# The second set's rows, turns and pair products inside the first set's inversion

## The chip, the cores and the metric

One core of a Trainium2 chip runs the kernel. The metric is the device time of one execution in microseconds, the median of several; an engine is TensorE (PE, with its weight loads as PEld), VectorE (DVE), ScalarE (ACT), GpSimd (POOL) or SyncE (SP, which here only issues DMAs).

## The reference

A recurrence over 768 steps for 4 batches x 8 heads, a 40 x 40 state each, and behind it two dense layers over the 3072 tokens of width 320 (hidden width 2048):

```python
for t in range(S):
    y[:, :, t] = np.einsum('bhd,bhde->bhe', rt, state)
    Sa = np.einsum('bhde,bhe->bhd', state, at)
    state = state * wt[:, :, None, :] - np.einsum('bhd,bhe->bhde', Sa, bt) + np.einsum('bhd,bhe->bhde', vt, kt)
h = x @ w_in                      # x: y as (3072, 320)
g = np.where(h >= 1, h, np.where(h <= -1, 0, (h + 1) ** 2 / 4))
out = g @ w_out
```

All data are fp32.

## The kernel before

The recurrence is done in 24 chunks of 32 steps (`L`). In a chunk the products of w up to each step turn the recurrence into matrix products: k and b are multiplied by the reciprocal products, a by the products (the rows `kt, P, at, bt`), and the steps' dependence on one another is a unit triangular 32 x 32 matrix for each head, made of the pair products of a and b, whose inverse `tinv` is needed. Four chunks are a set; there are six sets. For each set the rows are made, written to DRAM (`scr`), the pairs multiplied, the 32 x 32 matrices inverted (`invert`, 31 steps of a product L362 and a subtraction L368) and adopted by a transpose (L376).

The rows of sets 0 and 1 are made in one piece ahead of the loops (`early_rows`, a generator that the schedule advances): products of w (L172 to L177), a (L179, L180), reciprocals (L182, L184), then b and k (L186, L188). Their `at` and `bt` are turned on TensorE against an identity (`early_turn`, L199, four parts for each of the two), evicted by ScalarE (`early_evict`, L212), multiplied into pairs (`early_ab`, L223, evicted by L227) and stored chunk by chunk (`early_store`, L231, on SP's queue). r and v are copied to the same rows in DRAM by `copy_rv` (L138). Set 0 comes first, with its inversion on VectorE; set 1's inversion and those of the later sets are on GpSimd, a step at a time within windows.

The buffers of the early rows are borrowed: set 1's inputs lie in Xraw[0], Xraw[1], tiab and Yraw, its rows in wides[0] and its turned rows in wides[1], where set 0's rows were. The places of w_out's weights are opened later over both wides.

Every engine runs its instructions in the order in which the program writes them, and the whole order is written out by hand. `step_back("inv", 0)` advances set 0's inversion by a step (of 1, one VectorE instruction); the table `todo` says after which step something else is put in: `at(n, f)`. Behind the inversion comes the loop over chunks. In each chunk there are two halves of 16 heads (`hb`), each a `chain` of five stages: L519 with the copy L523; L529 with L536 and L540; L545 with L550, L556 with L563 and L568; L585 with L587. `turn` makes transposes on VectorE (L464, L467, L469), `scores` the products L485 and masks L497, `load_ti` and `load_cg` load the rows from DRAM, `shift` copies within a tile (L311). A chunk has four `fill`s. A fill has six slots; in each, the dense layers advance by 1280 columns (`feed`, once a group of 64 steps of y is there), one entry of the list `first` is taken (before: set 1's remaining rows, turns, pairs and stores), the weights advance by `PACE` steps (0.7 in the first ten fills, then 0.9), and the inversions, rows and pairs of later sets advance by their windows.

The dense layers run in 96 units (12 groups of tokens, eight each): `first` (L631), the gate (L639, L640, L642), a split into a rounded value and a rest (L648 on ScalarE, L649 on GpSimd) and `second` (L661). The weights arrive as eight-byte words whose bits are put together: a job (12 of w_in, 16 of w_out) is loaded raw on GpSimd's queue five jobs ahead (`AHEAD`, L711), two activations put its parts in staging places in Xraw (L723, L727), VectorE joins them (L731), ScalarE rounds (L743), and the rest is the subtraction L744, on VectorE for w_in and on GpSimd for w_out. Three pulls of `weights` are a job. The first unit needs 14 jobs done. With every third job of w_in L749 copies two parts on GpSimd's queue.

PSUM has four buffers for the recurrence (`psum`), two for `first` and two for `second`.

Of the kernel before, what the change touches and what calls it, by code (L numbers as in the profile page):

```python
# [9 lines left out]
F32 = mybir.dt.float32  # L10
# [23 lines left out]
AHEAD = 5  # L34
PACE = (0.7, 0.9)
# [19 lines left out]
def rwkv_moe_kernel(ctx: ExitStack, tc: tile.TileContext, r, k, v, w, a, b, w_in, w_out, ident_d, mask_d, out):  # L55
# [107 lines left out]
    def early_rows(s):  # L163
# [18 lines left out]
        nc.vector.reciprocal(rs[:, :, 7], Ps[:, :, 7])  # L182
        for t in range(7, 0, -1):
            nc.vector.tensor_mul(rs[:, :, t - 1], rs[:, :, t], ws[:, :, t])  # L184
        yield
        nc.vector.tensor_mul(bt, bl, rec)  # L186
        yield
        nc.vector.tensor_mul(kt, kl, rec)  # L188
# [158 lines left out]
    def invert(s):  # L347
# [5 lines left out]
        nc.gpsimd.memset(W, 0.0)  # L353
        nc.gpsimd.memset(W[:, 0:1024:33], 1.0)
# [359 lines left out]
    def weights():  # L714

        def start(k):
            m, n = sizes[k]
            words = raws[k][0:m]
            if jobs[k][0]:
                x, low = Xraw[1][0:m, n * ((k + 2) % 3) :][:, 0:n], Xraw[1][0:m, 3 * n : 4 * n]  # L720
            else:
                x, low = (y[0:m, n * ((k + 1) % 3) :][:, 0:n] for y in (Xraw[1], Xraw[0]))
# [14 lines left out]
        def split(k, x):  # L737
# [6 lines left out]
            (nc.gpsimd if kind else nc.vector).tensor_sub(lo, x, hi.bitcast(F32))  # L744
# [63 lines left out]
    load_ti(0, 1)  # L808
    for part in range(2):
        init_cg(1, part)  # L810
    load_cg(0, 1)
    for _ in range(2):
        next(rows_of[1])
    step_back("inv", 0)
    todo = {}
    at = lambda n, f: todo.setdefault(n, []).append(f)
    for c in range(1, 4):
        at(1, lambda c=c: early_store(0, c))
    for i in range(2):
        at(1, lambda i=i: copy_rv(0, i, 1, 3))  # L820
    for k in range(AHEAD):
        at(2, lambda k=k: raw_load(k))
# [5 lines left out]
    at(17, lambda: shift(0, 1))  # L828
    at(19, lambda: turn(0, 1, 0))
# [10 lines left out]
    gens = {}  # L840
# [3 lines left out]
    def turn_1(j, part):  # L844
        early_evict(1, j, part, early_turn(1, j, part))

    row = lambda: next(rows_of[1])
    steps = [[row], [], [row], [], [row], []]
    for part in range(4):
        steps[part + 1].append(lambda part=part: turn_1(0, part))  # L850
    steps += [[lambda part=part: turn_1(1, part)] for part in range(4)]
    steps += [[lambda half=half: early_ab(1, half)] for half in range(2)] + [[lambda: init_cg(2, 2)]]
    steps += [[lambda c=c: early_store(1, c)] for c in range(4)]
    steps += [[lambda i=i: copy_rv(1, i, 0, 4)] for i in range(2)] + [[lambda: pad_scr(1)]]
# [11 lines left out]

    def stage(c, hb):

        if (c, hb) in gens:
            next(gens[c, hb], 0)  # L870
# [103 lines left out]
```

## Time and profile before

| | us |
|---|---|
| median of 3 runs | 847.39 (845.87 to 848.33) |
| profiled execution, its own time | 853.33 |
| its span, first to last instruction | 851.4 |
| TensorE busy in it | 694.7 (82%) |
| VectorE | 592.5 (70%) |
| ScalarE | 477.5 (56%) |
| GpSimd | 444.8 (52%) |

The span has a start (the early rows, set 0's inversion to 64 us, three chunks without dense layers to some 152 us), a middle in which recurrence and dense layers share TensorE, and from about 800 us an end with dense layers alone. The profile gives for each instruction its start and duration and what ended the idle time of its engine before it. A share of busy time is a mean over stretches with different limits, so it is read by stretch.

### The profile page before, as it was taken

Reading aid. Unit: us, or ns where it says so; the run is one execution under the profiler, and the core shown is the slowest. Engines: PE = TensorE matmul, PEld = TensorE weight load, DVE = VectorE, ACT = ScalarE, POOL = GpSimd, SP = SyncE. Lnnn points to the kernel's source line nnn. Section 1 sums busy time; section 2 is a strip of 40 time slices with the busy share of each in tenths; the row PEclk is TensorE's granted clock in tenths of the full one; section 3 lists DMA queues with packets and bytes.
Section 4 is the critical chain, followed back from the end, with each engine's and each line's share of the span. In section 5 each row is a group of like instructions: output and inputs, shape, how many; then the busy total and the mean of one; then the engine's idle time right before and its main releaser. Section 6 shows DMA issues by size and latency. Waiting matters only on the chain.

```text
span 851.4 us, 35341 instructions
## 1 busy us (share of the span) xinstructions
PE 694.7 (82%) x15360; PEld 639.7 (75%) x15360; DVE 592.5 (70%) x1338; ACT 477.5 (56%) x1010; POOL 444.8 (52%) x623
## 2 busy tenths in 40 slices
PE   4334656687588867888998899999999999999994
PEld 4234645676577766778987789998899899999994
DVE  6796689978577845667777797787877678676210
ACT  5406466567554634545656466666566566655552
POOL 1300269986434777833778648775357743222331
PEclk9555566688887987878999899999999999999998
DMA  8798586875567545953538845434233334330100
GB/s 284 160 204 200 85 171 169 202 181 150 150 135 164 132 115 104 177 130 96 126 92 157 187 131 122 93 88 93 70 79 65 83 66 100 78 80 20 36 16 16
DMA packets 178450, 102.33 MB, mean 120 GB/s; under 512 B 123712, under 2 KB 171008, under 8 KB 178296
## 3 DMA queue, kind: packets, MB, share of 16 engines
q1 hardware_dynamic: 172024, 78.45, 42.3%
q0 software_dynamic: 6272, 21.63, 9.0%
q8 instruction: 121, 1.98, 1.0%
q14 instruction: 33, 0.27, 0.1%
HBM read 70.88 MB, written 27.53 MB: 116 GB/s over the span
## 4 chain that ended last, share of the span: by engine, by line
PE 49%; POOL 7%; DVE 6%; DMA 3%; ACT 3%; issue 2%; SPq 1%; ACTq 0%; POOLq 0%; DVEq 0%
PE ph L631 16%; PE po L661 15%; PE p L556 4%; PE p L545 3%; PE p L585 3%; PE p L485 2%; PE p L529 2%; PE p L519 2%; POOL lw L368 2%; POOL lw L362 2%; POOL gl L649 2%; PE p L334 1%; DMA lw<-scr 1%; DMA ld_w<-in_w_dram 1%; DMA scr<-arena 1%
## 5 line engine op out<-in xcount | busy, mean ns | idle before, releaser
L649 POOL TENSOR_TENSOR gl<-gt,gh 128x512 fp32r<-128x512 f32 x96 | 123.8, 1290 | 195.4 <-ACT gh L648 195.2
L631 PE MATMUL ph<-X,w 120*128 120x256 f32 x1536 | 222.8, 300 | 1.3 <-issue 1.3
L631 PEld LDWEIGHTS ph<-X,w 120*128 120x128 f32 x1536 | 202.3, 202 | 8.1 <-issue 1.3
L661 PE MATMUL po<-w,gh 128*128 128x320 f32 x768 | 134.4, 317 | 12.8 <-ACT gh L648 12.8
L642 DVE SCALAR_TENSOR_TENSOR gt<-gt,ph 128x512 f32<-128x512 f32 x96 | 65.6, 684 | 98.5 <-ACT gt L640 94.2
L661 PEld LDWEIGHTS po<-w,gh 128*128 128x128 f32 x768 | 117.5, 194 | 15.2 <-ACT gh L648 14.5
L639 ACT ACTIVATE gt<-ph,half_c 128x512 f32<-128x512 f32 x96 | 66.0, 688 | 65.3 <-PE ph L631 64.9
L661 PE MATMUL po<-w,gl 128*128 128x320 f32 x384 | 79.2, 330 | 19.7 <-POOL gl L649 19.7
L563 DVE SCALAR_TENSOR_TENSOR cg<-p,pr 40x160 f32<-40x160 f32 x184 | 59.1, 321 | 50.3 <-PE p L556 48.1
L368 POOL TENSOR_TENSOR lw<-lw 128x31 f32<-128x31 f32 (+15 forms) x155 | 88.5, 571 | 9.4
L362 POOL TENSOR_TENSOR lw<-lw 128x31 f32<-128x31 f32 (+15 forms) x155 | 82.7, 533 | 8.9
L497 DVE TENSOR_TENSOR cg<-p,mask 32x256 f32<-32x256 f32 x192 | 80.6, 420 | 3.5
L661 PEld LDWEIGHTS po<-w,gl 128*128 128x128 f32 x384 | 63.1, 199 | 24.1 <-POOL gl L649 23.7
L540 ACT ACTIVATE cg<-p 32x160 f32<-32x160 f32 x192 | 56.6, 295 | 40.1 <-PE p L529 22.1
L556 PE MATMUL p<-cg 128*64 128x72 f32 (+1 forms) x1536 | 66.4, 245 | 0.4 <-issue 0.4
L648 ACT CAST gh<-gt 128x512 fp32r<-128x512 f32 x96 | 59.6, 621 | 10.5 <-DVE gt L642 9.5
L550 ACT COPY ss<-p 40x320 f32<-40x320 f32 x92 | 38.6, 419 | 45.1 <-PE p L545 43.5
L640 ACT ACTIVATE gt<-gt 128x512 f32<-128x512 f32 x96 | 60.7, 632 | 3.1
L536 DVE SCALAR_TENSOR_TENSOR cg<-p,mask 32x128 f32<-32x128 f32 x192 | 55.3, 288 | 10.2 <-PE p L529 2.6
L556 PEld LDWEIGHTS p<-cg 128*64 128x64 f32 x1536 | 60.6, 154 | 0.9 <-issue 0.9
L585 PEld LDWEIGHTS p<-pr,ss 40*40 40x40 f32 x1472 | 36.1, 130 | 29.6 <-issue 25.2
L585 PE MATMUL p<-pr,ss 40*40 40x32 f32 x1472 | 41.2, 210 | 20.8 <-DVE pr L469 17.8
(97 smaller groups left out, 1121.2 us busy)
## 6 DMA issues: line engine op xcount, KB each, us to landing
ti<-scr SPq DMA_DIRECT2D x96, 200.0 KB
scr<-arena POOLq DMA_DIRECT2D x16, 640.0 KB, 5.6
cg<-scr SPq DMA_DIRECT2D x96, 80.0 KB
X<-Y SPq DMA_DIRECT2D x36, 160.0 KB
scr<-wide SPq DMA_DIRECT2D x8, 640.0 KB
w<-in_moe_w_out_dram POOLq DMA_DIRECT2D x16, 320.0 KB, 4.0
tiab<-scr SPq DMA_DIRECT2D x28, 160.0 KB
cg<-scr SPq DMA_DIRECT2D x96, 40.0 KB
```

The lines of the kernel that those rows point to most:

```text
L362: eng.tensor_mul(t3, W3[:, 0:n, j : j + 1].broadcast_to([128, n, m]), L3[:, j + 1 :, j].unsqueeze(1).broadcast_to([128, n, m]),)
L368: eng.tensor_sub(W3[:, 0:n, j + 1 :], W3[:, 0:n, j + 1 :], t3)
L497: nc.vector.tensor_tensor(out=cg[q, f::2, C_X : C_X + 64][:, 4 * i : 4 * i + 4].rearrange("p h (j x) -> p h j x", x=32), in0=ps[quarter(f, ...
L556: nc.tensor.matmul(psv[h // 8][64 * f : 64 * f + 64, h // 2 % 4, 0:n3], lhsT=cgw[:, h * CW + C_G : h * CW + C_G + 64], rhs=cg[:, h, C_R : ...
L585: nc.tensor.matmul(psv[er[f], p, :], lhsT=ss[er[f], p, :], rhs=pn[er[f], p, 0, 8:40], start=True, stop=True)
L631: nc.tensor.matmul(phs[k % 2][:, n * j : n * j + n], lhsT=wt[0, f // 4, wi // 2][:, wi % 2, fs], rhs=Xs[g][:, xi, :], start=i == 0, stop=i ...
L639: nc.scalar.activation(gt, ph, AF.Relu, bias=half_c, scale=0.5)
L640: nc.scalar.activation(gt, gt, AF.Square)
L642: nc.vector.scalar_tensor_tensor(out=gt, in0=gt, scalar=1.0, in1=ph, op0=ALU.min, op1=ALU.max)
L648: nc.scalar.copy(gh, gt)
L649: nc.gpsimd.tensor_sub(gl, gt, gh.bitcast(F32))
L661: nc.tensor.matmul(pos[i], lhsT=x[:, ts_], rhs=w, start=q == 0 and k == 0, stop=end)
```

## The change

Set 1's reciprocal products (L184) and its products with b and k (L186, L188) go to GpSimd, in nine pieces that are put in at steps 1 to 9 of set 0's inversion; its reciprocal (L182) is written just behind that inversion's first transpose. Its turns with their evictions are put in at steps 22 to 29 and its pair products at 58 and 60. In the loop their place in `first` is empty. Set 0's stores, and then the copies of r and v, are issued ahead of the inversion's steps, before the loads of chunk 0's second half; that half's shift comes at step 54 and its turn 0 in the loop. The first stage of chunk 0's first half comes at step 20. Set 1's stores are entries 12 to 15 of `first` (before 13 to 16), its copies of r and v 24 and 25 (before 17 and 18), and its one-row copy `pad_scr` is gone. Set 0's inversion has its start matrix made on ScalarE. The weights take 1.2 steps a slot in the first four fills, then 0.9; the subtraction of jobs 0 to 6 goes to GpSimd, and the staging places of w_in's jobs alternate between the two Xraw, four for one part and two for the other.

```diff
-PACE = (0.7, 0.9)
+PACE = (1.2, 0.9)
...
         nc.vector.reciprocal(rs[:, :, 7], Ps[:, :, 7])
+        eng = nc.gpsimd if s else nc.vector
+        if s:
+            yield
         for t in range(7, 0, -1):
-            nc.vector.tensor_mul(rs[:, :, t - 1], rs[:, :, t], ws[:, :, t])
+            eng.tensor_mul(rs[:, :, t - 1], rs[:, :, t], ws[:, :, t])
+            if s:
+                yield
+        if not s:
+            yield
+        eng.tensor_mul(bt, bl, rec)
         yield
-        nc.vector.tensor_mul(bt, bl, rec)
-        yield
-        nc.vector.tensor_mul(kt, kl, rec)
+        eng.tensor_mul(kt, kl, rec)
         yield
...
-        nc.gpsimd.memset(W, 0.0)
-        nc.gpsimd.memset(W[:, 0:1024:33], 1.0)
+        if s:
+            nc.gpsimd.memset(W, 0.0)
+            nc.gpsimd.memset(W[:, 0:1024:33], 1.0)
+        else:
+            zero(W)
+            nc.scalar.activation(
+                W[:, 0:1024:33], half_c.broadcast_to([128, 32]), AF.Copy, scale=2.0
+            )
...
-                x, low = (y[0:m, n * ((k + 1) % 3) :][:, 0:n] for y in (Xraw[1], Xraw[0]))
+                x, low = (Xraw[y][0:m, n * i : n * i + n] for y, i in (((1, 1), (0, 0), (1, 0), (0, 1))[k % 4], (1 - k % 2, 2)))
...
-            (nc.gpsimd if kind else nc.vector).tensor_sub(lo, x, hi.bitcast(F32))
+            (nc.gpsimd if kind or k < 7 else nc.vector).tensor_sub(lo, x, hi.bitcast(F32))
...
-    load_ti(0, 1)
-    for part in range(2):
-        init_cg(1, part)
-    load_cg(0, 1)
+    for c in range(1, 4):
+        early_store(0, c)
     for _ in range(2):
         next(rows_of[1])
     step_back("inv", 0)
+    for part in range(2):
+        init_cg(1, part)
+    load_ti(0, 1)
+    load_cg(0, 1)
+    for i in range(2):
+        copy_rv(0, i, 1, 3)
+    next(rows_of[1])
...
-    for c in range(1, 4):
-        at(1, lambda c=c: early_store(0, c))
-    for i in range(2):
-        at(1, lambda i=i: copy_rv(0, i, 1, 3))
-    for k in range(AHEAD):
-        at(2, lambda k=k: raw_load(k))
+    for k in range(9):
+        at(1 + k, lambda: next(rows_of[1]))
+        if k % 2 and k // 2 < AHEAD:
+            at(1 + k, lambda k=k: raw_load(k // 2))
+    for k in range(4, AHEAD):
+        at(6 + k, lambda k=k: raw_load(k))
...
-    at(17, lambda: shift(0, 1))
-    at(19, lambda: turn(0, 1, 0))
+    gens[0, 0] = chain(0, 0)
+    at(20, lambda: stage(0, 0))
+    for j in range(2):
+        for part in range(4):
+            at(22 + 4 * j + part, lambda j=j, part=part: turn_1(j, part))
+    at(54, lambda: shift(0, 1))
+    for half in range(2):
+        at(58 + 2 * half, lambda half=half: early_ab(1, half))
...
-    steps = [[row], [], [row], [], [row], []]
-    for part in range(4):
-        steps[part + 1].append(lambda part=part: turn_1(0, part))
-    steps += [[lambda part=part: turn_1(1, part)] for part in range(4)]
-    steps += [[lambda half=half: early_ab(1, half)] for half in range(2)] + [[lambda: init_cg(2, 2)]]
-    steps += [[lambda c=c: early_store(1, c)] for c in range(4)]
-    steps += [[lambda i=i: copy_rv(1, i, 0, 4)] for i in range(2)] + [[lambda: pad_scr(1)]]
+    steps = [[] for _ in range(3)] + [[lambda: init_cg(2, 2)]]
+    steps += [[] for _ in range(8)] + [[lambda c=c: early_store(1, c)] for c in range(4)] + [[] for _ in range(8)]
+    steps += [[lambda i=i: copy_rv(1, i, 0, 4)] for i in range(2)]
...
-            due[0] += PACE[now[0] >= 25]
+            due[0] += PACE[now[0] >= 10]
...
-            gens[c, 0] = chain(c, 0)
+            if c:
+                gens[c, 0] = chain(c, 0)
             gens[c, 1] = chain(c, 1)
         stage(c - 1, 1)
-        stage(c, 0)
+        if c:
+            stage(c, 0)
...
-            for j in (1, 2):
+            for j in (1, 2) if c else (1, 2, 0):
                 turn(c, 1, j)
```

## Rows read from the trace of the kernel before

**Rows 1.** Busy time in three stretches: PE, PEld, DVE, ACT, POOL, clock, DMA share.

```profile
34.00:64.00 30.00, 9.24 (x224) 8.11 (x224) 27.61 (x73) 3.53 (x8) 5.50 (x11) 0.56 1.00 209
64.00:85.00 21.00, 9.87 (x226) 8.71 (x226) 12.70 (x25) 14.85 (x28) 1.25 (x3) 0.57 0.85 202
...
500.00:600.00 100.00, 99.64 (x2449) 92.11 (x2447) 78.09 (x191) 64.50 (x143) 63.35 (x93) 0.98 0.46 107
```

**Rows 2.** Groups of instructions by line, VectorE, 33.55 to 61.7 us: busy, mean ns.

```profile
L368 DVE TENSOR_TENSOR lw<-lw 128x31 f32<-128x31 f32 (+15 forms) x31 | 10.6, 343 | 1.2
L362 DVE TENSOR_TENSOR lw<-lw 128x31 f32<-128x31 f32 (+15 forms) x31 | 10.6, 342 | 1.1
```

**Rows 3.** Timeline, 43 to 71 us: start, time, engine, instruction, what ended the wait.

```profile
43.74 0.90 DVE L464 STREAM_TRANSPOSE cg<-ti 64x256 f32<-64x256 f32 x2
...
61.73 1.91 DVE L376 STREAM_TRANSPOSE tinv<-lw 128x1024 f32<-128x1024 f32 x1
...
64.73 1.11 DVE L182 RECIPROCAL arena<-wide 128x160 f32<-128x160 f32 x1
65.87 2.48 DVE L184 TENSOR_TENSOR arena<-arena,X 128x160 f32<-128x160 f32 x7
...
70.17 0.45 PE L529 MATMUL p<-x,tinv 32*32 32x72 f32 x4 [17.42 <-ACT wide L212]
70.40 1.49 DVE L188 TENSOR_TENSOR wide<-Y,arena 128x1280 f32<-128x1280 f32 x1
```

**Rows 4.** Timeline, 77 to 91 us.

```profile
77.08 0.59 DVE L536 SCALAR_TENSOR_TENSOR cg<-p,mask 32x128 f32<-32x128 f32 x2 [0.30 <-ACT cg L540]
...
77.72 4.99 PE L199 MATMUL p<-pr,wide 128*40 128x64 f32 x96 [2.03 <-DVE cg L536]
...
90.27 0.95 PE L545 MATMUL p<-cg 128*40 128x40 f32 x21
```

**Rows 5.** Groups of instructions, ScalarE, whole span, shapes apart: busy, mean ns, idle before.

```profile
L212 ACT COPY wide<-p 40x512 f32<-40x512 f32 x16 | 9.3, 578 | 1.6 <-PE p L199 1.4
...
L727 ACT ACTIVATE X<-w 120x512 uint32<-120x512 uint8 x8 | 5.3, 663 | 20.4 <-DVE arena L184 20.4
```

**Rows 6.** Groups of instructions, GpSimd, whole span, shapes apart.

```profile
L649 POOL TENSOR_TENSOR gl<-gt,gh 128x512 fp32r<-128x512 f32 x96 | 123.8, 1290 | 195.4 <-ACT gh L648 195.2
...
L292 POOL TENSOR_TENSOR arena<-ld_b,wz 128x320 f32<-128x320 f32 x16 | 16.7, 1046 | 0.0
...
L368 POOL TENSOR_TENSOR lw<-lw 128x156 f32<-128x156 f32 x10 | 5.2, 520 | 0.6
```

**Rows 7.** VectorE's weight steps by shape; two of them and GpSimd's L649 in the timeline.

```profile
L731 DVE SCALAR_TENSOR_TENSOR X<-X 128x320 uint32<-128x320 uint32 x16 | 14.5, 908 | 2.6 <-ACT X L727 2.5
...
L731 DVE SCALAR_TENSOR_TENSOR X<-X,X 120x512 uint32<-120x512 uint32 x8 | 6.2, 779 | 0.0
L744 DVE TENSOR_TENSOR w<-X,w 120x512 fp32r<-120x512 f32 x8 | 6.0, 745 | 12.0 <-ACT w L743 11.9
...
179.89 3.24 DVE L731 SCALAR_TENSOR_TENSOR X<-X 128x320 uint32<-128x320 uint32 x1
183.76 0.49 DVE L731 SCALAR_TENSOR_TENSOR X<-X 128x320 uint32<-128x320 uint32 x1 [0.63 <-ACT X L727]
...
180.52 1.26 POOL L649 TENSOR_TENSOR gl<-gt,gh 128x512 fp32r<-128x512 f32 x1
```

**Rows 8.** TensorE in the timeline from 157 us; waits from 64 to 106 us.

```profile
157.21 1.54 PE L545 MATMUL p<-cg 128*40 128x40 f32 x31 [0.79 <-ACT cg L540]
...
171.21 1.43 PE L661 MATMUL po<-w,gl 128*128 128x320 f32 x4 [6.42 <-POOL gl L649]
...
POOL w L749 <- ACT w L743: 14.4, 1, 14.4
```

**Rows 9.** SP in the timeline; DMA issues, median us to landing last.

```profile
35.55 13.19 SPq L231 DMA_DIRECT2D scr<-wide  x3
...
w<-in_moe_w_in_dram POOLq DMA_DIRECT2D x16, 160.0 KB, 7.2
```

More of the change, by code (lines that the diff above doesn't have):

```diff
@@ L814, in rwkv_moe_kernel, with stage, turn_1 @@
     step_back("inv", 0)
+    for part in range(2):
[5 more added lines that the diff above has]
+    next(rows_of[1])
+    gens = {}
+    def stage(c, hb):
+        if (c, hb) in gens:
+            next(gens[c, hb], 0)
+    def turn_1(j, part):
+        early_evict(1, j, part, early_turn(1, j, part))
     todo = {}
     at = lambda n, f: todo.setdefault(n, []).append(f)
-    for c in range(1, 4):
-        at(1, lambda c=c: early_store(0, c))
-    for i in range(2):
-        at(1, lambda i=i: copy_rv(0, i, 1, 3))
-    for k in range(AHEAD):
-        at(2, lambda k=k: raw_load(k))
+    for k in range(9):
[4 more added lines that the diff above has]
+        at(6 + k, lambda k=k: raw_load(k))
     at(9, lambda: shift(0, 0))
@@ L839, in rwkv_moe_kernel @@
     mgen = moe()
-    gens = {}
     owed, idle = [0], [True]
@@ L843, in rwkv_moe_kernel @@
     due = [0]
-    def turn_1(j, part):
-        early_evict(1, j, part, early_turn(1, j, part))
-    row = lambda: next(rows_of[1])
-    steps = [[row], [], [row], [], [row], []]
-    for part in range(4):
-        steps[part + 1].append(lambda part=part: turn_1(0, part))
-    steps += [[lambda part=part: turn_1(1, part)] for part in range(4)]
-    steps += [[lambda half=half: early_ab(1, half)] for half in range(2)] + [[lambda: init_cg(2, 2)]]
-    steps += [[lambda c=c: early_store(1, c)] for c in range(4)]
-    steps += [[lambda i=i: copy_rv(1, i, 0, 4)] for i in range(2)] + [[lambda: pad_scr(1)]]
+    steps = [[] for _ in range(3)] + [[lambda: init_cg(2, 2)]]
+    steps += [[] for _ in range(8)] + [[lambda c=c: early_store(1, c)] for c in range(4)] + [[] for _ in range(8)]
+    steps += [[lambda i=i: copy_rv(1, i, 0, 4)] for i in range(2)]
     first = [lambda x=x: [f() for f in x] for x in steps]
@@ L865, in feed @@
             idle[0] = d is None
-    def stage(c, hb):
-        if (c, hb) in gens:
-            next(gens[c, hb], 0)
     def catch_up():
```

## The prediction, made before the changed kernel was run

> **What bounds the kernel now.** I read the busy time by stretch first [rows 1]. From 500 us on TensorE is busy 99.6 us in 100: whatever is won ahead of that arrives at the end unchanged, and nothing in the change touches what is done there. The start is different. From 34 to 64 us VectorE is busy 27.6 of 30 us, while TensorE, ScalarE and GpSimd do 9.2, 3.5 and 5.5: this is the first set's inversion on VectorE, 31 steps of a product and a subtraction at 0.34 us [rows 2], with the three others nearly idle beside it. From 64 to 85 no engine is busy for more than 71% of the time, so there something waits in a chain. The timeline [rows 3, 4] says what. The inversion's last transpose ends at 61.73 + 1.91 = 63.64 us. The next step of the recurrence on TensorE (L529) needs only that, but starts at 70.17: it has waited 17.4 us for the eviction L212 of the second set's turns, which stand ahead of it and hold the PSUM buffers. L212 stands on ScalarE behind L727, which writes a part of a staged weight into Xraw[0] and waited 20.4 us for L184, the second set's reciprocal products on VectorE: those read the same buffer and stand behind the inversion [rows 5]. After L529 the pattern repeats on TensorE: the masked results L536 are ready at 77.08 + 0.59 = 77.7, but L545, which takes them up, starts at 90.27, since 96 of the second set's turns (L199) and all its pair products (L223) are ahead of it in the queue. So 90.27 - 63.64 = 26.6 us pass between the end of the inversion and L545, and that is what the change attacks. After that come half-chunks of (157.21 - 90.27) / 5 = 13.4 us each [rows 4, 8] until the dense layers begin.
>
> **The change part by part.** The stretch from the inversion to L545. The turns, their 16 evictions and the pair products go inside the inversion, where TensorE and ScalarE are idle; the block of ScalarE at L727 falls away, since Xraw[0] is free earlier and the first job no longer stages there. I cost them at nothing: their cover is the inversion, some 28 us, against 9.3 us of evictions [rows 5] and less of TensorE. What remains from the last transpose to L545 is what stood from L529 to the end of L536 before, 77.7 - 70.2 = 7.5 us (it had two weight steps and one product L188 in it; now it has three transposes, one of them moved here, and two weight steps), and 0.7 for the copy: 8.2 us in place of 26.6, **-18.4**.
>
> The inversion itself gets longer. The reciprocal L182 now stands inside it, +1.11; the transposes of the other half's fifth array (0.90) leave it [rows 3]. The identity from which the inversion starts is made on ScalarE instead of GpSimd, while VectorE still transposes the pairs: nothing; if it came late, the inversion would wait some 1 us for it. The seven reciprocal products and the two large ones, 2.5 + 2 x 1.49 us on VectorE [rows 3], go to GpSimd. Their price there is not in the trace: for 128x160 the nearest row is 128x156 at 0.52; for 128x1280 I have 2.5 ns per element (128x512 in 1.29) and 3.3 (128x320 in 1.05) [rows 6], so 3.2 to 4.2 us each. These are contiguous operands, as in the first of the two rows: I take 3.3. The sum is 7 x 0.5 + 2 x 3.3 = 10.1 us, between 9.9 and 12.
>
> They are not free although GpSimd is idle. L731 on VectorE, two inputs from SBUF, took 0.49 us at 183.76 and 3.24 at 179.89, where GpSimd ran several tensor operations in a row, L649 from 180.52 to 181.78 among them [rows 7]. So one of the two stands still while the other works. No row has L362 or L368 of VectorE beside GpSimd, but they too have both inputs in SBUF, and the products fall among them. What GpSimd holds, VectorE loses, save where VectorE does something that doesn't collide: its transposes and masks in there: of the 28.1 us [rows 2] the two lines and the waits ahead of them take 10.6 + 10.6 + 2.3, so 4.6 are left, 3.7 without the transposes that leave. The cost is 6 to 12 us; below, 0 if these forms don't collide at all. I take **+8**, near 10.1, with half of the harmless work underneath. The Trainium skill (SBUF — State Buffer, Who interferes with whom) has it that any VectorE instruction with two SBUF inputs contends with a GpSimd instruction that reads SBUF, and that the loser is blocked for the whole instruction; that speaks against this change, takes L362 and L368 in with L731, and leaves out the end at 0; the 3.24 us agree. The Trainium skill (GPSIMD Engine Reference, 3.1 Elementwise — side-by-side cycle accounting) gives 4497 ns for 2048 elements, so an estimate of 2.8 us for 1280; by that the sum would be 1 us lower.
>
> Inversion: +1.1 - 0.9 + 8 = +8.2. L545 of the first half-chunk then comes 18.4 - 8.2 = 10.2 us earlier, near 80.
>
> Weights. PACE rises from 0.7 to 1.2 steps for the first four fills and is 0.9 for the rest: 7.2 and 5.4 steps per fill in place of 4.2, three steps to a job. After 4 fills 9.6 jobs are done instead of 5.6, after 10 fills (when the dense layers begin, and need 14) 20.4 instead of 14. The subtraction of jobs 0 to 6 goes to GpSimd. On VectorE, the busiest engine there, a job is L731 at 0.78 and L744 at 0.75 [rows 7]. Third and fourth fill: before 2.8 x 1.53 = 4.3; now 4.8 x 0.78 + 2.6 x 0.75 = 5.7: **+1.4** on the path. The next six: before 6.4 x 1.53 + 2 x 0.91 = 11.6; now 2.4 x 1.53 + 8.4 x 0.91 = 11.3: nothing. Behind the start of the dense layers 6.4 jobs fewer are left, 6.4 x 0.91 = 5.8 us of VectorE; TensorE waits only partly for it there, so I take **-2** of 0 to -6. The staging places go from three to four, so that a late subtraction on GpSimd holds ScalarE later: nothing, as long as GpSimd keeps up.
>
> Queues. On SP the first set's three stores (13.2 us of issuing [rows 9]) now stand ahead of the loads for the other half, which are wanted only at the end of the inversion: nothing. On GpSimd the first five weight loads stand between the products; they delay these by some 1 us a pair, while VectorE runs. The second set's stores keep about their place, its r and v copies come a fill or two later; they are wanted in chunk 4: nothing.
>
> The sum: -18.4 + 8.2 + 1.4 - 2 = **-10.8 us**. The profiled execution took 853.33 us (span 851.4 and 1.9 around it), 5.9 above the median 847.39. 853.3 - 10.8 - 5.9 = 836.6.
>
> **The rivals.** (a) The products hardly collide: GpSimd works while VectorE is between or in harmless instructions. Against it is the 3.24 us row; for it, that VectorE and GpSimd may alternate without loss. The inversion ends up to 8 us earlier, 828.6. (b) GpSimd becomes the bound. It gets seven subtractions of 1.29 more, 9.0 us, just ahead of the second set's inversion, and 6.4 jobs earlier. Already before, TensorE waited 6.4 us at 171.2 for its product L649 [rows 8]. Against it: before, GpSimd stood still for 14.4 us behind one cast, just ahead of that inversion [rows 8]. If 8 of the 9.0 arrive at L649, 844.6. (c) Slower: the weights outrun their transfers. A job every 2.8 us is wanted in the first four fills (13.4 / 2 = 6.7 us each, 2.4 jobs); a load lands a median of 7.2 us after its issue [rows 9], five are under way, so it holds as long as a landing takes under 5 x 2.8 = 14 us. The DMA engines were busy all of 34 to 64 and 85% of the next 21 us [rows 1], and the second set's stores fall into the same stretch. If loads come one at a time, each of the 4.6 jobs beyond the first five waits 7.2 - 2.8 = 4.4, 20.2 us in all, since ScalarE stands at L723 with the recurrence's copies behind it: 836.6 + 20.2 = 856.8. (d) The change doesn't do it: the evictions of the second set stand behind its DMA reads or products so long that TensorE still has them in front of L529; then the 18.4 shrink to about the inversion's 8.2 and the time stays at 847.
>
> **How the numbers follow.** Forecast 0.45 (832 to 841), (a) 0.15, (b) 0.2, (c) 0.13, (d) 0.07. 0.3% is 2.5 us, about what a measurement can tell here: faster means below 844.9, slower above 849.9. Faster: 0.45 + 0.15 + 0.6 of (b) = 0.72; within: the rest of (b), (d) = 0.15; slower: 0.13. The range leaves out most of (c), and the better half of (a): 826 to 849.
>
> **What would show it.** In the trace of the changed kernel: the last transpose of the inversion (L376 before) ends near 72 us instead of 63.6, with instructions of L362 and L368 of several us where GpSimd's large products run; no instruction of these lengthened would be (a). The evictions L212 into wide lie inside the inversion. L529 follows the transpose within 1 us, and L545 within 10; L727 no longer waits 20 us. The first L631, just ahead of 157.21 before, comes 9 to 12 us earlier. A wait of ScalarE for weight loads in 70 to 110 us would be (c); L649 waited for by TensorE for more than the 6.4 us, (b). I am wrong if the gain at the first L545 isn't there any more at the first L631, or if the dense layers wait longer than before.

## The result

The changed kernel takes 835.97 us (835.47 to 838.92), the kernel before beside it 847.86: a ratio of 0.9871, with a 95% interval of 0.9842 to 0.990. The prediction was 836.6. The profiled execution took 835.64 us with a span of 833.9, against 853.33 and 851.4; this pair lies 17.5 us apart, the medians 11.9, since the execution of before that was profiled lies 5.5 us above its median. One execution differs from the next by some us on its way, so a stage is read with care where the differences are no larger than that, and times are compared by their medians. Lines have moved: those from L190 to L352 of the kernel before stand 6 further down in the changed kernel, those from L360 to L800 12. So L362, L368, L376 are now L374, L380, L388; L529, L536, L540, L545, L556, L585 are L541, L548, L552, L557, L568, L597; L631 and L649 are L643 and L661; L711 (raw loads) is L723, and L723, L727, L731, L743, L744 are L735, L739, L743, L755, L756; L199, L212, L223, L231, L311 are L205, L218, L229, L237, L317, and L311 is now the load of `ti`. The second set's reciprocal products are L187 on GpSimd, its large products L192 and L194.

The timeline of the changed kernel around the inversion (start, duration, engine, instruction; the rows of before are [rows 3, 4]):

```profile
33.31 0.12 DVE L374 TENSOR_TENSOR lw<-lw 128x31 f32<-128x31 f32 x1
...
33.47 1.17 POOL L187 TENSOR_TENSOR arena<-arena,X 128x160 f32<-128x160 f32 x2 [29.11 <-DVE lw L374]
...
40.83 2.88 POOL L192 TENSOR_TENSOR wide<-tiab,arena 128x1280 f32<-128x1280 f32 x1
40.97 2.93 DVE L374 TENSOR_TENSOR lw<-lw 128x175 f32<-128x175 f32 x1
43.65 1.09 POOL L723 DMA_DIRECT2D w<-in_moe_w_in_dram  x2
43.93 3.92 DVE L380 TENSOR_TENSOR lw<-lw 128x175 f32<-128x175 f32 x1
44.76 2.89 POOL L194 TENSOR_TENSOR wide<-Y,arena 128x1280 f32<-128x1280 f32 x1
...
68.84 1.97 DVE L388 STREAM_TRANSPOSE tinv<-lw 128x1024 f32<-128x1024 f32 x1
...
77.69 1.54 PE L557 MATMUL p<-cg 128*40 128x40 f32 x31 [3.83 <-ACT cg L552]
```

Two instructions of the inversion that take 0.34 us elsewhere last 2.93 and 3.92 us, and end when GpSimd's L192 and L194 end. The inversion ends at 70.81 instead of 63.64, and L557, which was L545 at 90.27, stands at 77.69. The second set's 16 evictions and its pairs are done by 69.6. Busy time by stretch (PE, PEld, DVE, ACT, POOL, granted clock, DMA share; [rows 1] before):

```profile
34.00:64.00 30.00, 12.61 (x354) 11.63 (x354) 28.21 (x53) 11.08 (x21) 14.51 (x20) 0.63 0.80 158
64.00:85.00 21.00, 9.84 (x446) 8.62 (x446) 16.18 (x40) 13.71 (x29) 7.39 (x11) 0.56 0.54 137
500.00:600.00 100.00, 98.31 (x2365) 90.12 (x2366) 76.15 (x183) 62.89 (x141) 58.90 (x89) 1.00 0.42 94
```

ScalarE now does 11.1 us beside the inversion instead of 3.5, GpSimd 14.5 instead of 5.5. So far it is as forecast. What follows isn't. TensorE's timeline, first of the kernel before ([rows 4, 8] have more of it), then of the changed one:

```profile
102.31 1.54 PE L545 MATMUL p<-cg 128*40 128x40 f32 x31 [2.37 <-ACT cg L540]
...
115.39 1.54 PE L545 MATMUL p<-cg 128*40 128x40 f32 x31 [0.80 <-ACT cg L540]
...
152.65 3.78 PE L631 MATMUL ph<-X,w 120*128 120x256 f32 x16
...
182.62 0.81 PE L545 MATMUL p<-cg 128*40 128x40 f32 x32
```

```profile
95.22 1.54 PE L557 MATMUL p<-cg 128*40 128x40 f32 x31 [4.65 <-ACT cg L552]
...
111.72 1.54 PE L557 MATMUL p<-cg 128*40 128x40 f32 x31 [2.72 <-ACT cg L552]
...
151.16 1.62 PE L643 MATMUL ph<-X,w 120*128 120x256 f32 x6 [1.61 <-DMA X<-Y]
...
169.55 1.43 PE L673 MATMUL po<-w,gl 128*128 128x320 f32 x4 [6.92 <-POOL gl L661]
...
180.64 0.81 PE L557 MATMUL p<-cg 128*40 128x40 f32 x32
```

The half-chunks from 77.69 to 111.72 take 17.5 and 16.5 us, where before they took 12.0 and 13.1. The first product of a dense layer is 1.5 us ahead of before, not 10, and at 180.64 TensorE is 2.0 us ahead (182.62 before). Then the lead comes back. Numbering the half-chunks from 0 and taking the first matrix product of the last-but-one stage (L556 before) as the mark of each, the changed kernel leads as follows:

| half-chunk | 0 | 2 | 4 | 6 | 8 | 9 | 10 | 16 | 24 | 47 |
|---|---|---|---|---|---|---|---|---|---|---|
| before, us | 92.8 | 116.7 | 143.3 | 183.3 | 220.3 | 246.4 | 269.8 | 385.0 | 507.7 | 795.9 |
| after, us | 79.0 | 113.0 | 137.7 | 181.3 | 210.4 | 231.2 | 254.1 | 366.5 | 488.8 | 778.3 |
| lead, us | 13.9 | 3.7 | 5.7 | 2.0 | 9.8 | 15.2 | 15.7 | 18.5 | 18.9 | 17.6 |

Of the 17.6 us at the end, some 5.5 are the excess of the profiled execution of before. A time that agrees to 0.6 us stands on steps two of which were far off. The experiments ask which part of the change takes the lead away and which gives it back.

### The profile page after: what moved, and what is told of

Same layout as the page of the kernel before. It is cut to its first block, busy times and chain, and to the rows that moved or that the text cites. A ratio compares the mean times of both kernels' runs of the same rounds, so it can differ in the third digit from the quotient of the medians.

```text
span 833.9 us, 35334 instructions
## 1 busy us (share of the span) xinstructions
PE 683.6 (82%) x15360; PEld 628.6 (75%) x15360; DVE 585.9 (70%) x1322; ACT 479.8 (58%) x1012; POOL 461.9 (55%) x637
## 4 chain that ended last, share of the span: by engine, by line
PE 51%; POOL 6%; DVE 6%; DMA 4%; ACT 3%; issue 2%; SPq 1%; ACTq 0%; POOLq 0%; DVEq 0%
PE ph L643 17%; PE po L673 16%; PE p L568 4%; PE p L557 3%; PE p L597 3%; PE p L497 3%; PE p L541 2%; PE p L531 2%; POOL lw L380 2%; POOL lw L374 1%; POOL gl L661 1%; PE p L340 1%; DMA ld_w<-in_w_dram 1%; DMA lw<-scr 1%; DMA scr<-arena 1%
## 5 line engine op out<-in xcount | busy, mean ns | idle before, releaser
L661 POOL TENSOR_TENSOR gl<-gt,gh 128x512 fp32r<-128x512 f32 x96 | 123.7, 1288 | 197.1 <-ACT gh L660 196.9
L643 PE MATMUL ph<-X,w 120*128 120x256 f32 x1536 | 222.8, 300 | 3.0 <-DMA X<-Y 1.6
L643 PEld LDWEIGHTS ph<-X,w 120*128 120x128 f32 x1536 | 201.8, 201 | 10.4 <-issue 3.8
L380 POOL TENSOR_TENSOR lw<-lw 128x31 f32<-128x31 f32 (+15 forms) x155 | 88.6, 572 | 9.4
L673 PE MATMUL po<-w,gl 128*128 128x320 f32 x384 | 77.0, 323 | 20.3 <-POOL gl L661 20.3
L374 POOL TENSOR_TENSOR lw<-lw 128x31 f32<-128x31 f32 (+15 forms) x155 | 81.0, 523 | 8.7
L673 PEld LDWEIGHTS po<-w,gl 128*128 128x128 f32 x384 | 61.3, 194 | 24.8 <-POOL gl L661 24.5
L552 ACT ACTIVATE cg<-p 32x160 f32<-32x160 f32 x192 | 56.5, 294 | 36.3 <-PE p L541 22.1
L548 DVE SCALAR_TENSOR_TENSOR cg<-p,mask 32x128 f32<-32x128 f32 x192 | 55.2, 287 | 15.6 <-ACT cg L552 7.9
L568 PE MATMUL p<-cg 128*64 128x72 f32 (+1 forms) x1536 | 64.7, 242 | 1.5 <-issue 1.5
L597 PE MATMUL p<-pr,ss 40*40 40x32 f32 x1472 | 42.1, 212 | 26.3 <-DVE pr L481 26.3
L597 PEld LDWEIGHTS p<-pr,ss 40*40 40x40 f32 x1472 | 36.9, 132 | 35.1 <-issue 18.8
L568 PEld LDWEIGHTS p<-cg 128*64 128x64 f32 x1536 | 58.9, 150 | 2.0 <-issue 2.0
```

The source lines that it names most:

```text
L374: eng.tensor_mul(t3, W3[:, 0:n, j : j + 1].broadcast_to([128, n, m]), L3[:, j + 1 :, j].unsqueeze(1).broadcast_to([128, n, m]),)
L380: eng.tensor_sub(W3[:, 0:n, j + 1 :], W3[:, 0:n, j + 1 :], t3)
L568: nc.tensor.matmul(psv[h // 8][64 * f : 64 * f + 64, h // 2 % 4, 0:n3], lhsT=cgw[:, h * CW + C_G : h * CW + C_G + 64], rhs=cg[:, h, C_R : ...
L597: nc.tensor.matmul(psv[er[f], p, :], lhsT=ss[er[f], p, :], rhs=pn[er[f], p, 0, 8:40], start=True, stop=True)
L643: nc.tensor.matmul(phs[k % 2][:, n * j : n * j + n], lhsT=wt[0, f // 4, wi // 2][:, wi % 2, fs], rhs=Xs[g][:, xi, :], start=i == 0, stop=i ...
L661: nc.gpsimd.tensor_sub(gl, gt, gh.bitcast(F32))
```

## The experiments

All marks below are those of the table above: the half-chunk's number, and the time in us from the span's start. "Inversion" is the stretch from the first L362 to the end of the adopting transpose (30.0 us before, 37.5 after).

| run | inversion | 0 | 1 | 2 | 3 | 6 | 10 | 16 | span | median, us | ratio to before (95%) |
|---|---|---|---|---|---|---|---|---|---|---|---|
| before | 30.0 | 92.8 | 103.6 | 116.7 | 130.7 | 183.3 | 269.8 | 385.0 | 851.4 | 847.86 | 1 |
| after | 37.5 | 79.0 | 96.5 | 113.0 | 125.2 | 181.3 | 254.1 | 366.5 | 833.9 | 835.97 | 0.9871 (0.9842 to 0.9900) |
| e13, after again | 37.5 | 79.2 | 99.1 | 115.5 | 127.7 | 183.9 | 256.7 | 369.2 | 833.7 | 835.46 | 0.9848 (0.9815 to 0.9880) |
| e1, old pace | 37.3 | 77.4 | 89.0 | 101.0 | 119.9 | 172.6 | 258.3 | 373.0 | 840.6 | 838.01 | 0.9852 (0.9826 to 0.9878) |
| e2, before with new pace | 30.0 | 99.5 | 112.7 | 129.7 | 141.8 | 198.0 | 272.7 | 385.8 | 849.3 | 850.03 | 1.0001 (0.9982 to 1.0020) |
| e3, products on VectorE | 32.6 | 76.9 | 96.0 | 112.5 | 124.6 | 180.6 | 253.4 | 365.2 | 829.6 | 835.94 | 0.9826 (0.9799 to 0.9852) |
| e4, rests on VectorE | 37.5 | 79.6 | 97.5 | 114.6 | 126.7 | 182.9 | 256.9 | 370.9 | 838.2 | 836.82 | 0.9846 (0.9820 to 0.9871) |
| e5, stores early | 37.5 | 78.6 | 94.5 | 111.7 | 123.9 | 180.0 | 253.2 | 365.0 | 830.0 | 832.46 | 0.9807 (0.9753 to 0.9860) |
| e7, turns in the loop | 37.4 | 94.4 | 107.2 | 123.7 | 135.9 | 191.9 | 266.2 | 378.1 | 844.4 | 845.64 | 0.9965 (0.9950 to 0.9980) |
| e8b, no low part | | 77.9 | 96.1 | 112.5 | 124.7 | 180.8 | 253.6 | 365.3 | 832.5 | 834.29, one | |
| e9, no joining | | 76.8 | 93.4 | 108.3 | 122.6 | 176.3 | 251.2 | 360.9 | 826.8 | 828.56, one | |
| e12, narrow jobs | 37.5 | 76.9 | 89.7 | 108.7 | 123.4 | 177.1 | 250.4 | 361.7 | 825.7 | 827.46, one | |
| e10, VectorE, stores early | 32.5 | 77.6 | 93.6 | 110.9 | 123.0 | 179.2 | 253.7 | 366.0 | 833.1 | 833.29 | 0.9818 (0.9785 to 0.9852) |
| e11, and old pace, copies late | 32.5 | 77.5 | 89.0 | 99.3 | 112.2 | 168.3 | 254.9 | 368.0 | 834.4 | 835.17 | 0.9836 (0.9804 to 0.9869) |

The second profile of the changed kernel tells the grain of such a reading: 2.5 us later than the first from half-chunk 1 to 18, and level with it at the end.

### Does the pace of the weights matter?

```diff
 e1, on the changed kernel
-PACE = (1.2, 0.9)
+PACE = (0.7, 0.9)
...
-            due[0] += PACE[now[0] >= 10]
+            due[0] += PACE[now[0] >= 25]
 e2, on the kernel before: the opposite edit
```

> The changed kernel with the old pace of the weights (0.7 steps a slot for ten fills, then 0.9), all else as changed. Theory 1 (the prediction's): the gain is made at the inversion and the pace matters little: about 837 us, and the 13.9 us by which the first half-chunk is ahead of before stay. Theory 2 (the pace takes the front's gain and repays it): the third half-chunk stays 10 us or more ahead of before instead of 3.7, but the half-chunks 7 to 10 no longer win 13 us, so 840 to 846 us. Theory 3 (GpSimd pins the start of the dense layers): half-chunk 6 is at 181 to 184 us whatever the pace, and the end lies at 836 plus what the later jobs cost.

> The kernel before with the new pace alone (1.2, from the fifth fill on 0.9). Theory 1: 848 within 2 us. Theory 2: the first half-chunks are later than before by 5 to 10 us, the half-chunks 7 to 10 win it back and more: 840 to 846 us. Theory 3: half-chunk 6 later than before's 183 us by the jobs that GpSimd gets earlier, and the end at 845 to 850.

By the marks theory 2 came out on both kernels; by the times it did not, since it expected 840 to 846 us for both and they are 838.01 and 850.03, near theory 1's 837 and 848: what is taken comes back, and no more. Without the new pace the lead over before stays: 15.4 us at half-chunk 0, 15.7 at 2, 10.7 at 6. With it, 12.0 of them are gone at half-chunk 2 (113.0 against 101.0) and 8.7 at 6. On the kernel before the new pace alone costs 13.0 us at half-chunk 2 (129.7 against 116.7) and 14.7 at 6. And it is paid back: from half-chunk 6 to 16 the changed kernel takes 185.3 us with the new pace and 200.4 with the old one; the kernel before takes 201.8 and, with the new pace, 187.8. The sums are near nothing: e2 1.0001, e1 0.9852 where the changed kernel has 0.9871 and 0.9848. Up to half-chunk 2 the new pace has 11 jobs joined instead of 7, in both pairs, so a job costs 12.0 / 4 = 3.0 and 13.0 / 4 = 3.3 us of the recurrence there; behind half-chunk 6 there is 1 job left instead of 8, and 15.1 / 7 = 2.2 and 14.0 / 7 = 2.0 us come back for each. The pace moves the price of a job; it saves little or nothing of it.

The marks of e1 have one exception, half-chunk 3: from 2 to 3 it takes 18.9 us. Its waits from 98 to 122 us (who waited for whom: us, times, longest), and SP's timeline:

```profile
ACT ti L317 <- DMA ti<-scr: 6.9, 2, 6.4
DVE cg L548 <- ACT cg L552: 6.4, 2, 6.2
PEld p L557 <- ACT cg L552: 5.4, 1, 5.4
```

```profile
92.42 11.25 SPq L138 DMA_DIRECT2D scr<-in_v_dram  x1
103.78 5.59 SPq L311 DMA_DIRECT2D ti<-scr  x2
```

SP stands 11 us in issuing the second set's copy of v, the loads of the next rows queue behind it, and ScalarE's shift waits for them. The changed kernel has the same row (94.32, 12.52 us), but its ScalarE is late anyway: it has no wait for `ti` from 92 to 130 us. The kernel before holds the same loads back as long, in the one-row copy that stood behind that of v,

```profile
101.08 10.01 SPq L144 DMA_DIRECT2D scr<-in_r_dram  x1
```

and there too nothing waits for them, since the recurrence is 15 us later than in e1.

### GpSimd and VectorE in the inversion

```diff
 e3, on the changed kernel, early_rows
-        eng = nc.gpsimd if s else nc.vector
+        eng = nc.vector
```

> The changed kernel with the second set's products on VectorE, in the same places inside the inversion. The nine products take 2.5 + 2 x 1.5 = 5.5 us there, against the 8.4 us by which the inversion grew beside GpSimd, if GpSimd and VectorE shut each other out; no instruction of the inversion lasts over 0.5 us, and it ends 2.5 to 3 us earlier than 70.8 us. If the growth had another cause (the transfers, the pace of ScalarE's evictions), it ends 5 us later. Time: 833 if the start carries to the end; 836 if what lies behind it is pinned by GpSimd.

No instruction of the inversion lasts over 0.43 us any more, and it is 32.6 us long: 5.0 shorter than with the products on GpSimd, 2.6 longer than before. VectorE's timeline:

```profile
36.63 0.33 DVE L187 TENSOR_TENSOR arena<-arena,X 128x160 f32<-128x160 f32 x1
36.87 0.22 DVE L374 TENSOR_TENSOR lw<-lw 128x60 f32<-128x60 f32 x1
37.00 0.32 DVE L187 TENSOR_TENSOR arena<-arena,X 128x160 f32<-128x160 f32 x1
37.24 0.21 DVE L380 TENSOR_TENSOR lw<-lw 128x60 f32<-128x60 f32 x1
```

Product and inversion alternate, and each starts 0.1 us before the one ahead of it is over: the products fill gaps that two dependent instructions leave. So the two engines do shut each other out, the work is cheaper on the busy engine than on the idle one, and the growth isn't owed to transfers. But the end doesn't show it (835.94 against 835.97). 2.9 of the 5.0 us are lost ahead of the inversion, which starts at 36.2 here, 36.9 in e10 and 38.4 in e11, and at 32.3 to 33.6 in the eleven other profiles. Two stretches (columns as above), TensorE, and one of SP's issues, first of the changed kernel, then of e10:

```profile
0.00:10.00 10.00, 0.27 (x4) 0.22 (x4) 4.50 (x14) 5.45 (x3) 3.83 (x12) 1.00 0.78 275
...
20.00:27.00 7.00, 3.54 (x255) 3.16 (x255) 4.73 (x13) 3.47 (x7) 0.00 (x0) 0.91 0.60 152
...
21.10 1.22 PE L205 MATMUL p<-pr,wide 128*40 128x64 f32 x35 [1.63 <-issue]
...
29.04 0.75 PE L229 MATMUL p<-cg,lw 40*32 40x32 f32 x36 [3.25 <-issue]
...
7.80 2.63 SPq L144 DMA_DIRECT2D scr<-in_r_dram  x1
```

```profile
0.00:10.00 10.00, 0.41 (x4) 0.22 (x4) 4.64 (x14) 5.45 (x3) 8.09 (x20) 1.00 0.77 277
...
20.00:27.00 7.00, 3.66 (x127) 3.30 (x127) 2.95 (x8) 2.88 (x6) 0.00 (x0) 0.68 1.03 331
```

```profile
22.25 2.01 PE L205 MATMUL p<-pr,wide 128*40 128x64 f32 x35 [2.78 <-issue]
...
28.59 1.93 PE L229 MATMUL p<-cg,lw 40*32 40x32 f32 x128 [1.44 <-issue]
32.59 0.75 PE L229 MATMUL p<-cg,lw 40*32 40x32 f32 x36 [2.07 <-issue]
...
11.40 7.30 SPq L144 DMA_DIRECT2D scr<-in_r_dram  x1
```

With nothing of the second set on GpSimd, its first weight loads, which stood behind the products, are issued in the first 10 us (20 entries instead of 12), and their packets fall on 8 to 20 us instead of 37 to 53. SP then stands 7.30 us in L144 instead of 2.63, and asks for the second set's inputs from 18.75 us on instead of 10.48. These inputs fall on 20 to 27 us, where the transfers rise from 152 to 331 GB/s, and TensorE's pair products L229 come later. Ahead of the inversion it has "issue" waits in both kernels (it waits for nothing that the profile shows); those of over 0.7 us come to 4.9 us in the changed kernel and 6.3 in e10, to 6.5 in e3 and 9.1 in e11. What it waits for can be told from the packets in the traces: in all fourteen profiles each of these waits ends 1.2 to 1.5 us behind the end of a 16 KB packet of the queue that carries instructions. The last of these packets there ends at 26.8 to 28.8 us in the eleven profiles with the loads behind, and at 30.5, 31.1 and 32.9 in e3, e10 and e11. So it is TensorE's instructions that are late. That they are late because of the transfers beside them is an inference; no run holds the loads back alone.

### Rests of the weights on VectorE

```diff
 e4, on the changed kernel
-            (nc.gpsimd if kind or k < 7 else nc.vector).tensor_sub(lo, x, hi.bitcast(F32))
+            (nc.gpsimd if kind else nc.vector).tensor_sub(lo, x, hi.bitcast(F32))
```

> The changed kernel with all rests of w_in's jobs on VectorE again. Theory 1: VectorE bounds the chunks ahead of the dense layers, seven more subtractions of 0.7 us: 1 to 3 us slower. Theory 3: GpSimd is rid of 9 us ahead of the second set's inversion, which starts earlier than 103.6 us and ends earlier than 183.5; half-chunk 6 comes 3 to 8 us earlier and so does the end.

GpSimd is rid of seven subtractions, but the second set's inversion on it starts at 105.1 us instead of 103.6 and ends at 185.3 instead of 183.7; half-chunk 6 is 1.6 us later. In all fourteen profiles half-chunk 6 stands 1.5 to 2.5 us ahead of the end of that inversion, which lasts 75 to 85 us whatever stands beside it, and in e1 both come some 9 us earlier: the order of the program ties the two, GpSimd doesn't pin TensorE. Theory 3 falls. The 1 to 3 us of theory 1 can't be told from the spread, nor can the 836.82.

### Turns and pair products in the loop

```diff
 e7, on the changed kernel
-    for j in range(2):
-        for part in range(4):
-            at(22 + 4 * j + part, lambda j=j, part=part: turn_1(j, part))
...
-    for half in range(2):
-        at(58 + 2 * half, lambda half=half: early_ab(1, half))
...
+    steps = [[]] + [[lambda part=part: turn_1(0, part)] for part in range(4)] + [[]]
+    steps += [[lambda part=part: turn_1(1, part)] for part in range(4)]
+    steps += [[lambda half=half: early_ab(1, half)] for half in range(2)]
```

> The changed kernel with the second set's turns and pair products back in the loop, where they stood before; its products stay on GpSimd inside the inversion. If the gain of the start is that they left TensorE's queue ahead of L557 (the prediction's step): the inversion ends near 71 us as in the changed kernel, L541 follows at once, since ScalarE no longer stands at L739, but L557 comes 10 to 13 us later than 77.7, at 88 to 91; the time is 843 to 849. If the gain is only that ScalarE no longer stands still (L739): L557 stays within 4 us of 77.7 and the time within 3 us of the changed kernel's.

TensorE's timeline:

```profile
70.22 1.29 PE L541 MATMUL p<-x,tinv 32*32 32x72 f32 x32 [13.62 <-DVE tinv L388]
...
78.60 4.38 PE L205 MATMUL p<-pr,wide 128*40 128x64 f32 x96 [1.97 <-ACT cg L552]
...
90.51 1.70 PE L229 MATMUL p<-wide 40*32 40x32 f32 x107 [2.19 <-issue]
92.14 0.95 PE L557 MATMUL p<-cg 128*40 128x40 f32 x21
```

L541 follows the inversion at once, and yet L557 comes at 92.14, 14.5 us behind the changed kernel's and later than either answer, with the turns and the pairs ahead of it as in [rows 4]. Not all of the 14.5 is theirs: five jobs of weights are joined at half-chunk 0 here, two in the changed kernel. From half-chunk 1 on, where the counts agree, e7 is 10.6 to 11.0 us behind up to half-chunk 6, within the 10 to 13 that were expected. The time is 845.64, 0.9965: of the whole gain 9.7 us by the medians hang on these two moves.

### The second set's stores

```diff
 e5, on the changed kernel
-    steps = [[] for _ in range(3)] + [[lambda: init_cg(2, 2)]]
-    steps += [[] for _ in range(8)] + [[lambda c=c: early_store(1, c)] for c in range(4)] + [[] for _ in range(8)]
+    steps = [[lambda c=c: early_store(1, c)] for c in range(4)]
+    steps[3].append(lambda: init_cg(2, 2))
+    steps += [[] for _ in range(20)]
```

> The changed kernel with the second set's four stores at the first four slots of the loop instead of slots 12 to 15 (its copies of r and v stay). The prediction costs their place at nothing: 836 within 2 us. If the stores' place is what keeps the transfers of the next chunk and the weights clear (the DMA engines are busy throughout 85 to 106 us in the changed kernel), the loads for chunk 1 and the weights come later and the first three half-chunks lose 3 to 8 us; 838 to 843.

Neither: SP issues the stores at 56 us, while the inversion runs, and the half-chunks are 0.4 to 2.0 us earlier, not later, which is within the grain. 832.46 is the lowest median among the kernels that leave nothing out, but its interval (0.9753 to 0.9860) holds 0.9848; that the later place does no good is shown, that it does harm isn't.

### What a job costs

```diff
 e8b, on the changed kernel: w_in's jobs 2 to 11 without the second activation
-            nc.scalar.activation(
+            if jobs[k][0] or k < 2:
+              nc.scalar.activation(
                 low, words.bitcast(U8).rearrange("p (n b) -> p n b", b=8)[:, :, 3], AF.Copy, bias=-15.5 / 32, scale=1.0 / 32
             )
 e9, on the changed kernel: w_in's jobs without the joining
-            nc.vector.scalar_tensor_tensor(
+            if jobs[k][0]:
+              nc.vector.scalar_tensor_tensor(
                 out=x.bitcast(U32), in0=x.bitcast(U32), scalar=3, in1=low,
 e12, on the changed kernel: w_in's jobs with 32 columns in activations and joining
+                n, words = 32, words[:, 0:64]
...
+                nc.scalar.copy(hi, Xraw[k % 2][0:m, 0:n])
+                nc.gpsimd.memset(lo.bitcast(F32), 0.0)
```

> The changed kernel without ScalarE's second activation (L739) in w_in's jobs 2 to 11, 10 x 0.66 us less on ScalarE: the words' low part isn't made for them. If ScalarE's share is what a job costs the recurrence ahead of the dense layers, half-chunk 5 (156.1 us in the changed kernel) comes 5 us or more earlier; if VectorE's is, less than 2 us.

> The changed kernel without VectorE's joining (L743) in w_in's 12 jobs, 12 x 0.7 us less on VectorE and no waiting of ScalarE's rounding for it: the two parts of the words are not put together for them. If VectorE's share is what a job costs, or ScalarE's wait for it, half-chunk 5 comes 6 us or more earlier than 156.1; if ScalarE's own time is, less than 3 us.

> The changed kernel with w_in's 12 jobs cut to 32 of 512 columns in both activations and the joining, a plain full-width copy for the rounding, and a fill for the rest: their loads stay, most of their work on VectorE, ScalarE and GpSimd's reading of SBUF goes; the weights are not put together. If the work of the jobs on the three engines together is what the recurrence waits for ahead of the dense layers, half-chunk 2 comes 7 to 11 us earlier than 113.0; if their transfers or SP's queue are, it stays within 3 us.

6.6 us less on ScalarE (e8b) change nothing at half-chunk 5 (156.2 against 156.1). 8 us less on VectorE (e9) bring 3.1 us at half-chunk 1, 4.7 at 2, 3.4 at 5: between the two answers. These are single profiles, and measured against e13, the changed kernel's second one, the gain at half-chunk 5 would be 3.3 us for e8b and 6.8 for e9; so a part of ScalarE's is not excluded. Taking most of the work away on all three (e12) brings 6.8 us at half-chunk 1, nearly all of the 7.5 us by which the new pace is later there than the old one (96.5 against 89.0), but only 4.3 at half-chunk 2, outside both answers. From half-chunk 2 on e9 is as far ahead as e12 (5.6 and 4.8 us at 16), so the joining, with ScalarE's wait for it, is the largest single part found. The waits tell where the rest goes; in this order, the changed kernel and e9 from 79 to 113 us, and e12 from 89 to 110:

```profile
ACT w L755 <- DVE X L743: 6.8, 5, 2.2
...
ACT X L735 <- DMA w<-in_moe_w_in_dram: 3.5, 3, 1.6
```

```profile
ACT X L735 <- DMA w<-in_moe_w_in_dram: 7.0, 3, 3.8
```

```profile
ACT ti L317 <- DMA ti<-scr: 6.9, 2, 5.9
```

What one engine is spared becomes a wait for the raw weights (3.5 us, then 7.0), and without most of the work the recurrence's own loads are late (6.9 us). Busy time from half-chunk 0 to 2, in the changed kernel and in e1 (columns as above):

```profile
79.00:96.50 17.50, 8.06 (x232) 7.18 (x229) 12.47 (x27) 11.70 (x25) 14.26 (x20) 0.50 1.13 283
96.50:113.00 16.50, 8.09 (x232) 7.20 (x229) 13.17 (x29) 11.22 (x24) 11.02 (x22) 0.50 1.13 240
```

```profile
77.40:89.00 11.60, 7.79 (x232) 6.91 (x229) 11.23 (x25) 8.27 (x19) 7.72 (x12) 0.65 1.09 283
89.00:101.00 12.00, 7.58 (x234) 6.74 (x230) 9.36 (x24) 9.26 (x21) 10.39 (x18) 0.64 1.15 234
```

Over the two, VectorE works 5.1 us more, ScalarE 5.4 and GpSimd 7.2, none of them as much as the 10.4 us by which the stretch is longer (on the kernel before, e2 adds 3.7, 5.1 and 2.8 us of work, and 6.3 us of time). TensorE's granted clock is 0.50, its lower level of 1.2 GHz throughout, against means of 0.65 and 0.64, but TensorE is busy only 0.8 us longer, so the clock doesn't explain it. The reading that fits best is that no single engine sets the price of a job: it stands in the order of three engines between the steps of the recurrence, and where they are freed, the transfers are next. No run takes it apart fully.

### Two and three parts undone

e10 is e3 and e5 together; e11 is e10 with e1's edit and 36 instead of 20 empty slots ahead of the copies of r and v.

> The changed kernel with two of its parts undone: the second set's products on VectorE (inside the inversion), and its stores at the first four slots of the loop. If the two gains of the single runs are real and add up, the inversion ends near 68.5 us, half-chunk 2 is 2 us ahead of the changed kernel's 113.0, and the time is 3 to 6 us under that of the changed kernel run beside it. If either was the spread of the measurement, it is within 2 us of it.

> As the one before, and the old pace of the weights, with the copies of r and v 16 slots later, so that SP doesn't stand in them (11 to 12 us) ahead of the loads of chunk 1's second half. If the pace only moves the price of a job from one place to another (theory 2): half-chunk 6 near 167 us, 13 us ahead of the changed kernel, half-chunk 10 at 250 to 256, and the time within 2 us of the run with the new pace. If the copies cost 5 us of their own, 4 to 6 us under it.

e10's inversion ends at 69.4 us (late by its start), half-chunk 2 is 2.1 us ahead, and the median is 2.2 us under the changed kernel's beside it, with intervals that overlap: no version that is shown to be better. e11 shows the parts most clearly. Half-chunk 6 stands at 168.3, 15.0 us ahead of before, and 2 to 3 takes 12.9 us instead of e1's 18.9: the copies of r and v ahead of the loads cost 6 us there, as much as ScalarE's wait for them in e1. But half-chunk 10 is at 254.9, level with the changed kernel, and the time is 835.17. What the start wins over the changed kernel, 13.0 us at half-chunk 6, goes into jobs of weights that are still to be done.

> The changed kernel itself, beside the runs above on one chip: 0.987 of the kernel before, within 0.003, by both theories; a look at how much one execution differs from another in the trace.

It came out at 0.9848, and its trace is the grain told above.

## Why the prediction was right, and where its steps were not

**The stretch from the inversion to L545** was put at -18.4. It is 77.69 - 70.81 = 6.9 us instead of 26.6: -19.7. That this is the turns' and pairs' place in TensorE's queue, and not ScalarE's wait alone, e7 shows (with them in the loop L557 comes 14.5 us later, and 10.7 us stay from half-chunk 1 on). Right.

**The inversion** was put at +8.2, of which 8 for GpSimd and VectorE shutting each other out. Its stretch grew from 30.01 to 37.49, and 0.9 had left it: 8.4 for the products. The 1.1 for the reciprocal L182 stands ahead of that stretch (from 32.29 us), where an earlier first transpose made it up in this pair; so the inversion ends 7.2 us later. The large ones took 2.88 and 2.89 us, below the row-based 3.2 to 4.2 us and near the estimate of 2.8 from the Trainium skill (GPSIMD Engine Reference, 3.1 Elementwise — side-by-side cycle accounting); that alternation with GpSimd costs VectorE almost the whole of their time agrees with the Trainium skill (SBUF — State Buffer, Who interferes with whom), though the second of the two long instructions had begun 0.83 us ahead of L194 and still ended behind it. The sum came out since the smaller price met a larger loss: VectorE lost 2.9 + 3.9 - 0.7 = 6.1 us to the two alone. Rival (a) is refuted. Right, with the two halves off by about a microsecond.

**The weights ahead of the dense layers** were put at +1.4 on the path, from VectorE's 0.78 and 0.75 us per job. This step failed: 10.4 us between half-chunk 0 and 2 (34.0 us against e1's 23.6). A job costs the recurrence 3.0 to 3.3 us there, not 1.5 or less. I had priced the busiest engine's busy time, in a stretch where no engine is busy throughout. The likely cause is that a job takes two activations, the joining, the rounding and the rest one behind the other in engines that also carry the recurrence's copies, with the raw loads and SP's queue next in line; e9 and e12 show parts of it, and what each part costs stays open. The six fills behind, put at nothing, did take as long: from half-chunk 2 to 6 68.3 us in e10 and 69.0 in e11.

**The weights behind** were put at -2. This failed as far in the other direction: 185.3 us from half-chunk 6 to 16 against e1's 200.4, -15.1. TensorE did not wait "only partly": each job left over costs 2 us.

The two errors are of one cause and cancel. Added, they were -0.6 in the sum; e2 (1.0001) and e1 (0.9852) say about 0 by the medians, and the pair of profiles -6.7, of which 4.7 are the spread (e1's profiled execution, 842.36, lies 4.4 us above its median). The total was right because the pace is nearly neutral, which I had only as a small number plus a small number: to that extent the agreement is luck.

**Queues** were put at nothing. The first set's copies of r and v stand behind the loads for chunk 0's other half, not ahead of them as the section on the change has it; nothing hangs on that. The second set's copies hold SP for 11 to 12 us ahead of the loads of chunk 1, and 6 us of the recurrence with the old pace (e1 against e11); in the changed kernel that hides under the weights. The stores' place is worth nothing that can be measured. The weight loads between the products, which I called a delay of 1 us a pair, seem to be held back to good effect: e3, e10 and e11 let them go and start the inversion 2.9 to 5.1 us later, with TensorE's instructions late.

**Rivals.** (b) did not decide: TensorE's wait for GpSimd's L661 (L649 before) is 6.92 us against 6.42, and half-chunk 6 does not move with GpSimd's load (e4). (c) was partly there, though small: ScalarE waited 3.5 us for raw weights from 79 to 113 us, far from the 20.2 of that case. (d) fell with L557 at 77.69. What I said would show me wrong did happen: at the first L631 (L643) the gain was 1.5 us, not 9 to 12. It happened without moving the end, and the prediction had no step for a debt that is paid back.

## What to carry to other kernels

Work moved off a queue is worth what stood behind it there; work that is only done earlier or later costs about the same in either place, so price it by a run of instructions through all the engines it passes, not by the busiest one. An idle GpSimd is no free place beside a VectorE that reads two operands from SBUF: here the same nine products cost 8.4 us of the inversion on GpSimd and 3.5 on VectorE. And look at what waits behind a moved instruction on its own queue: when the products left GpSimd, the loads behind them went out 30 us earlier, and 2.9 of the 5.0 us won in the inversion were lost ahead of it.

## What the runs showed of the hardware

- An instruction of VectorE with two SBUF inputs waited for a whole GpSimd instruction that reads SBUF: 0.34 us became 2.93 beside one of 2.88. The next one, of the same size, began at 43.93, while GpSimd issued two DMAs (43.65 to 44.74) and 0.83 us ahead of L194, and still ended behind it, after 3.92 us; why it wasn't done before L194 began is not settled. Beside GpSimd's short products (0.54 to 0.6 us each) they alternated, most of VectorE's at 0.4 to 0.7 us in place of 0.2 to 0.3.
- Independent instructions put between dependent ones on VectorE overlapped them: 5.2 us of products made the inversion 3.5 us longer (32.6 - 30.0 + 0.9 us of transposes that had left).
- SP stood 11 to 13.4 us in one issue of a 640 KB copy from DRAM to DRAM in 160-byte pieces (the changed kernel, e1, e3, e13) and 5.1 to 5.2 us in e5 and e11. In the kernel before that issue took 0.61 us, and the copy of a single row behind it 10.01.
- Ahead of the inversion TensorE's "issue" waits of over 0.7 us ended 1.2 to 1.5 us behind a 16 KB packet of the instruction queue, in all fourteen profiles: 27.6 and 29.0 us in the changed kernel, 31.1 and 32.6 in e10.
